# Layer-norm tokens of the MLP turned by transposing DMAs, and VectorE's score row chosen by ScalarE's passes

## The chip, the cores and the metric

The kernel runs on one core of a Trainium2 chip. The metric is the device time of one launch in microseconds (us). The names used are PE for the matmul engine (TensorE), with PEld for its weight loads, DVE for VectorE, ACT for ScalarE, POOL for GpSimd and SP for the engine that issues the DMAs.

## The reference, cut to what matters

One transformer block with adaptive layer norm: 2048 tokens of width 512, 32 heads of width 16, an MLP of width 1376, all in bf16.

```python
mod = (silu(c) @ w_mod).reshape(1, 6, 1, 512)      # sa, ca, ga, sb, cb, gb
h = layernorm(x) * (1 + ca) + sa
q, k, v = split_heads(h @ A_wqkv)
p = softmax(q @ k.T * 16 ** -0.5)
x = x + ga * (merge_heads(p @ v) @ A_wo)
h = layernorm(x) * (1 + cb) + sb                   # the layer norm that the change touches
x = x + gb * (gelu(h @ B_w1 + B_b1) @ B_w2 + B_b2)
```

Attention has 32 x 2048 x 2048 = 134 million exponentials, and that is most of the work.

## The kernel before, in words

**Tiles.** The tokens form four blocks of 512. A run is four heads of one query block: its scores, transposed (128 keys by 512 queries per head), come from matmuls that use 32 rows of the PE array each, so four "rows" 0 to 3 (one per head) can run beside each other. There are 32 runs; each goes over 16 key tiles. The last query block is split in two halves of 256 queries.

**Two makers of exponentials.** ACT takes most scores: `qk_a` fills three PSUM banks, then two, then three (`st`), and one ACT instruction at L852 turns them into bf16 `pt`. These are 626 passes. DVE takes up to four key tiles of a run: `qk_d` lets PE write one head's row (128x512) into one of the two PSUM banks `ax`, and DVE at L900 adds a constant and writes it as int16 `ph`, which read as bf16 is roughly an exponential. Three shifted copies of that (`ph`, `sh`, at L953) and a last one (`sl`, at L932 on DVE and at L938 on POOL) are added up by PE, so that the error averages out. PE multiplies all of these with V (L994, accumulator `od`).

**After a run** `normalise` copies `od` to `OD`, sends the row sums through DRAM with SP's DMAs (`dn`, `dc`, `rn`, `RB`, at L1025 to L1040), and POOL multiplies (`OT`, `OS`, at L1046). When the eight runs of a query block are done, `block_tail` makes the rest of that block: `Wo` (L1155), the residual on DVE (`xb`, L1204), `layer_norm`, `W1` (L1217) with its eviction into `g` or `gp` on DVE (L1221), Gelu on ACT (L1232, L1226), `W2` (L1161), the output sum on DVE (L1244) and SP's store. There are four such tails: three of four token tiles, and one of two tiles, for the first half of the last block. The last two token tiles are made by `last_half`, a chain of its own at the very end.

**The layer norm of a tail** (`layer_norm`, the branch that is not for a tuple of PSUM pools): DVE takes the statistics of each token tile (L599), POOL the reciprocal root, DVE writes the normalised tokens `z` in bf16 (L610, tokens on partitions). PE then turns `z` with an identity matrix: for each of the four 128-wide slices of the width, one transpose per token tile (L672) into an `ax` bank. DVE modulates from PSUM into `h` (tile name `blk`): times 1 + cb, plus sb (L618). `h` is what `W1` reads.

**What sets the order.** The kernel is built by a planner in Python. Each piece of work is an `Op` with an engine, an assumed duration, what it depends on, and a priority. `Plan.step` always commits the operation that can start first on any engine, by assumed times; among those that could start within a small slack of the first, the one with the lowest priority value (`dyn`) goes. So every engine gets a fixed list in the order of the plan, and on the chip each engine runs its list in order, with semaphores. A few rules matter here:
- At most two of `qk_a`'s and two of `qk_d`'s score groups may wait for their maker (`n_a`, `n_d`). `dyn` gives a DVE score 1.0 if none waits and 7.0 if one does; a lower value goes first. An ACT score has 0.0, 2.2 or 6.0.
- Which of a DVE tile's remaining rows is written next is chosen in `Plan.commit` (L190), among `o.rows`.
- Work of the tails on PE gets due times spread over the runs that follow; it goes when nothing pressing is there.
- `SEEDS` (L57) has one number per 12.5 us of planned time. It adds a small pseudo-random term to the priorities, so a different seed gives a different order.
- DVE and POOL operations marked `port=True` are not planned beside each other.
- `heat` adds matmuls on a tile of zeros (L432, L437, L448) where the plan sees PE idle too long.
- DMAs of the planner are all issued by SP, in order.

Of the kernel before, what the change touches and what calls it, by code (L numbers as in the profile page):

```python
# [14 lines left out]
BF16 = mybir.dt.bfloat16  # L15
# [32 lines left out]
PEL = 0.24  # L48
# [5 lines left out]
AL = 0.31  # L54
FILL = 1.6
SPREAD = 0.3
SEEDS = (0, 0, 302, 271, 373, 425, 577, 466, 663, 322, 33, 746, 998, 229, 962, 365, 101, 777, 989, 946, 149, 601, 669, 525, 0, 671, 855, 955, 207, 0, 854, 454, 337, 529, 0, 291, 253, 66, 861, 627, 47, 810, 486, 485, 381, 714, 242, 531, 122, 22, 0, 676, 851, 0, 0, 0, 998, 0, 175, 0, 0, 0, 0, 0, 0, 0)  # L57
HEAT = 1.45


# [39 lines left out]
class Plan:  # L100
# [79 lines left out]
    def commit(self, s, o):  # L180
        self.lists[o.eng].remove(o)
        self.now = s
        if o.acq is not None:
            o.slot = min(range(len(o.acq.free)), key=lambda i: o.acq.free[i])
            o.acq.free[o.slot] = 1e18
            o.tile = o.acq.alloc(o.slot)
        if o.kind == "pv" and s >= self.cool and o.last_left() > 1:
            o.extra, o.us = True, 2 * o.us
        if o.rows is not None:
            o.row = min(o.rows, key=lambda i: self.tiles.get(i, 0.0) if self.mode == "qk" else i)  # L190
            o.mode = ("qk", o.row)
        if o.eng == "PE":
            self.done.append((s, o.act if o.act is not None else (o.us if o.mode[0] != "qk" else o.us * (len(o.mode) - 1) / 4)))
            while self.done[0][0] < s - 30.0:
                self.done.popleft()
            tot = 0.0
            self.fill_at = self.cool = 0.0
            for t, us in reversed(self.done):
                tot += us
                if tot >= HEAT and not self.cool:  # L200
                    self.cool = t + WIN
                if tot >= self.fill:
                    self.fill_at = t + WIN
                    break
            if o.mode[0] != self.mode:
                self.mode, self.tiles = o.mode[0], {}
            for i in o.mode[1:]:
                self.tiles[i] = s + o.us
            self.free["PE"] = s + 0.01
        else:  # L210
            self.free[o.eng] = s + o.us
            if o.port:
                self.port[o.eng] = s + o.us
            if o.eng == "DVE" and o.us > 0:
                self.dve = (s, s + o.us, o.port)
        o.end = s + o.us + o.lat
        if o.kb:
            q = "SP"
            self.bus[q] = max(self.bus[q], s + o.us + 0.9) + o.kb / (300.0 if s < 12.0 else 260.0)
            o.end = self.bus[q] + 0.7  # L220
        if o.fn is not None:
            o.fn(o)
        for owner in o.rel:
            owner.uses -= 1
            owner.last = max(getattr(owner, "last", 0.0), o.end + (DVE_PE if o.eng == "DVE" else 0.0))
            if owner.uses == 0:
                owner.acq.free[owner.slot] = owner.last
        for w in o.waiters:
            w.todo -= 1
            w.ready = max(w.ready, o.end + (DVE_PE if o.eng == "DVE" and w.eng == "PE" else 0.0))  # L230
            if w.todo == 0:
                self.lists[w.eng].append(w)
# [21 lines left out]
def kernel(  # L254
# [94 lines left out]
    def dyn(plan, o):  # L349
        if o.eng == "DVE" and o.run is not None and (  # L350
                o.run < a_run[0] or o.run == a_run[0] and not own[o.run]):
            return 0.05
        if o.eng != "PE":
            return o.prio
        same = (-0.5 if o.mode[0] == plan.mode else 0.0) - 0.2 * o.cont
        if o.kind == "qkA":
            back = n_a[0] - n_a[1]
            return (0.0 if back == 0 else 2.2 if back == 1 else 6.0) + same
        if o.kind == "qkD":
            back = n_d[0] - n_d[1]  # L360
            return (1.0 if back == 0 else 7.0) + same
        if o.kind == "pv":
            if units[0] == NR * NT * 4:
                return 0.0
            few = any(sum(f <= plan.now + 0.3 for f in p.free) <= FEW for p in r_pt)
            return (0.2 if few else 3.0) + same
        if o.kind in urgent:
            return 0.5 + same
        if o.kind == "last":
            return o.prio + 0.1 * same  # L370
        if o.due <= prog():
            return (2.5 if o.due + 16 > prog() else 0.8 if o.due + 48 > prog() else 0.3) + same
        return (4.0 if plan.now >= aux_at[0] else 8.0) + same
# [5 lines left out]
    TAIL, CB = 185, 49  # L379
    TAIL2, TAIL3 = 100, 60  # L380
    plan = Plan(dyn, later)
    plan.need = lambda: plan.free["ACT"] + sum(queued)
    due_now = [1e9, 0.0]

# [242 lines left out]
    def layer_norm(src, deps, mod, mod_dep, hold_z, alloc_h, engines, ps_res, kind, prio,  # L627
                   after=None, nt=TPB):

        ln = op("NIL", None, 0.0, (), lat=0.0, prio=0.0, acq=r_ln)  # L630
        st = [op("DVE", lambda o, t=t: stats(ln, t, src(t)), 0.83, (deps[t], ln, after and after[t]), prio=prio)
              for t in range(nt)]
        rs = [op("POOL", lambda o, i=i: rstd(ln, 2 * i, 2 * i + 2), 1.3,
                 st[2 * i:2 * i + 2] + [o_mh], prio=0.0) for i in range(nt // 2)]
        z = op("NIL", None, 0.0, (rs[0], hold_z), lat=0.0, prio=0.0, acq=r_z)
        za = [op("DVE", lambda o, t=t: apply(ln, z, t, src(t)), 0.33, (z, rs[t // 2]), prio=prio,
                 rel=(ln,), port=True) for t in range(nt)]
        h = op("NIL", None, 0.0, (rs[0],), lat=0.0, prio=0.0, acq=alloc_h)
        done = []
        trs = []  # L640
        if isinstance(ps_res, tuple):
            two = []
            for part in range(2):
                for half in range(2):
                    def tr(o, half=half, part=part):
                        if part:
                            o.tile = two[half].tile
                            two[half].ps = o.tile.bitcast(BF16)
                        ps = o.tile.bitcast(BF16)
                        for j in (2 * half, 2 * half + 1):  # L650
                            for t in (2 * part, 2 * part + 1):
                                nc.tensor.transpose(
                                    out=ps[:, (j % 2) * QB + t * P:(j % 2) * QB + (t + 1) * P],
                                    in_=z.tile[:, t, j * P:(j + 1) * P], identity=ident)
                    one = op("PE", tr, 4 * 0.0705, za[0:2 + 2 * part] + [o_id] + two[half:half + part],
                             lat=PEL, mode=("full", 0), kind=kind,
                             acq=None if part else ps_res[half], rel=(z,))
                    two.append(one)
            trs += two[2:4]
            for half in range(2):  # L660
                one, done_tr = two[half], two[2 + half]
                for j in (2 * half, 2 * half + 1):
                    e = engines[j]
                    done.append(op(e, lambda o, j=j, e=e, one=one: modulate(
                        e, h.tile[:, j, :], one.ps[:, (j % 2) * QB:(j % 2 + 1) * QB], mod, j),
                        0.5 if e == "DVE" else 0.72, (done_tr, mod_dep, h), prio=0.2, rel=(one,)))
        else:
            for j in range(NC):
                def tr(o, j=j):
                    o.ps = o.tile.bitcast(BF16)[:, 0:nt * P]  # L670
                    for t in range(nt):
                        nc.tensor.transpose(out=o.ps[:, t * P:(t + 1) * P],  # L672
                                            in_=z.tile[:, t, j * P:(j + 1) * P], identity=ident)
                one = op("PE", tr, nt * 0.0705, za, lat=PEL, mode=("full", 0), kind=kind,
                         acq=r_ax, rel=(z,))
                trs.append(one)
                e = engines[j]
                done.append(op(e, lambda o, j=j, one=one, e=e: modulate(
                    e, h.tile[:, j, 0:nt * P], one.ps, mod, j), 0.13 + nt * 0.1, (one, mod_dep, h), prio=0.1,
                    rel=(one,)))  # L680
        return h, done, za, trs


# [825 lines left out]
```

## Time and profile before

| | |
|---|---|
| three runs | 776.52, 776.95, 782.23 us (median 776.95) |
| profiled execution, its own time | 780.45 us |
| its span | 778.7 us |
| TensorE clock granted, mean over the span | 0.991 |
| first ACT pass `pt<-st` starts at | 15.1 us |
| PE transposes `ax<-ident,z` at L672 | 56, of 0.219 us each, from 339.3 to 731.9 us |
| DVE modulates of the tails, L618 | 12 of 128x512, 4 of 128x256, all from PSUM |
| Gelu passes over a whole block, L1232 | 3, of 4.9 us, each between two table loads of 1.28 us |
| SP's DMA of a 16x512 row, `qm<-qs` | 0.58 us to issue |

How to read it: a line of a group gives the code line, the engine, the operation, the tile written and the tiles read, the shape, the count, then the busy time, the mean of one instruction in ns, and the idle time of that engine just before these instructions, with what ended it. A line of the view by stretch gives for each engine the busy time and the number of instructions in that stretch, then the granted clock (1.00 is full), the DMA share and GB/s. Instructions on one engine overlap a little, so the step from start to start is shorter than the duration.

### The profile page before, as it was taken

How to read it: one execution, taken by the hardware profiler on the slowest of the kernel's cores; microseconds unless marked ns; L12 is line 12 of the kernel's file. 1: busy time of each engine (PE TensorE's matmuls, PEld its weight loads, DVE VectorE, ACT ScalarE, POOL GpSimd, SP SyncE). 2: the span in 40 equal slices, each digit the busy share in tenths (PEclk: the TensorE clock that was granted, in tenths of full speed). 3: DMA queues.
4: the chain of work that ended last, by engine and by line, in shares of the span. 5: the costliest groups of instructions: out<-in, count | busy, mean ns of one | idle time of the engine just before them, and what ended most of it. 6: DMA issues, size and time to landing. Idle time of an engine off the chain costs nothing.

```text
span 778.7 us, 20637 instructions
## 1 busy us (share of the span) xinstructions
PE 729.6 (94%) x8281; PEld 273.5 (35%) x8281; DVE 715.2 (92%) x1185; ACT 751.0 (96%) x679; POOL 279.4 (36%) x619
## 2 busy tenths in 40 slices
PE   8889989999999899999999999999999899999998
PEld 3433333233243222332322233232334344434454
DVE  6779898999999999999999889979999999998974
ACT  4999999999999999999999999999999999999994
POOL 6222434444433334444444333323234333232320
PEclk9999999999999999999998899999999999999999
DMA  7043001000011101000000100001110000110100
GB/s 216 31 144 85 19 24 44 26 12 16 19 46 51 23 21 50 19 22 28 22 25 17 29 20 23 19 22 31 31 49 24 25 18 18 45 31 11 52 19 28
DMA packets 39074, 28.23 MB, mean 36 GB/s; under 512 B 17957, under 2 KB 34374, under 8 KB 38978
## 3 DMA queue, kind: packets, MB, share of 16 engines
q1 hardware_dynamic: 38970, 26.91, 12.0%
q8 instruction: 65, 1.06, 0.5%
q14 instruction: 31, 0.25, 0.1%
q10 hardware_dynamic: 8, 0.00, 0.0%
HBM read 21.30 MB, written 2.61 MB: 31 GB/s over the span
## 4 chain that ended last, share of the span: by engine, by line
ACT 53%; PE 24%; DVE 12%; issue 9%; DMA 1%; POOL 0%; SPq 0%; DVEq 0%; ACTq 0%
ACT pt L852 52%; PE od L994 8%; PE st L803 7%; DVE ph L900 5%; PE ax L1217 2%; DVE sh L953 2%; PE ax L1161 2%; DVE ph L953 1%; PE t L1161 1%; PE ax L803 1%; PE ax L693 1%; DMA blk<-in_w_mod_dram 1%; DVE xb L1204 1%; PE t L1346 1%; ACT g L1232 1%
## 5 line engine op out<-in xcount | busy, mean ns | idle before, releaser
L852 ACT ACTIVATE pt<-st 128x1536 bf16<-128x1536 f32 x626 | 709.4, 1415 | 6.0 <-PE st L803 4.5
L900 DVE TENSOR_SCALAR ph<-ax 128x512 int16<-128x512 f32 x484 | 318.4, 684 | 23.6 <-PE ax L803 18.8
L938 POOL TENSOR_TENSOR sl<-ph,step 128x128 int32<-128x128 int32 x356 | 163.4, 461 | 335.7 <-DVE sh L953 95.0
L803 PE MATMUL st<-qm,kT 32*128 32x512 bf16 x1564 | 247.7, 385 | 32.7 <-ACT pt L852 26.6
L803 PEld LDWEIGHTS <-kT 32*128 32x128 bf16 x2048 | 86.0, 91 | 247.8 <-issue 237.4
L803 PE MATMUL ax<-qm,kT 32*128 32x512 bf16 x484 | 162.2, 382 | 2.6 <-DVE ph L900 1.7
L994 PEld LDWEIGHTS <-VEB 128*32 128x32 bf16 x4992 | 109.9, 96 | 150.6 <-issue 127.7
L994 PE MATMUL od<-pt,VEB 128*32 128x512 bf16 (+1 forms) x1952 | 149.0, 344 | 0.4 <-DVE OD L1019 0.2
L953 DVE TENSOR_SCALAR sh<-ph 128x4096 int16<-128x4096 int16 x121 | 146.8, 1215 | 1.2 <-PE od L994 0.9
L994 PE MATMUL od<-ph,VEB 128*32 128x512 bf16 (+1 forms) x1216 | 91.6, 341 | 1.3 <-DVE OD L1019 0.5
L994 PE MATMUL od<-sh,VEB 128*32 128x512 bf16 (+1 forms) x1216 | 84.9, 341 | 0.7 <-DVE sh L953 0.6
L953 DVE TENSOR_SCALAR ph<-ph 128x2048 int16<-128x2048 int16 x121 | 83.4, 691 | 0.5
L932 DVE TENSOR_SCALAR sl<-ph 128x1024 int16<-128x1024 int16 (+3 forms) x121 | 58.4, 488 | 0.6
L1046 POOL TENSOR_TENSOR OT<-OD,RB 128x128 bf16<-128x128 f32 x76 | 34.5, 457 | 61.0 <-DVE sh L953 40.7
L994 PE MATMUL od<-sl,VEB 128*32 128x512 bf16 (+1 forms) x608 | 49.1, 342 | 1.9 <-DVE sl L932 1.2
L1217 PE MATMUL ax<-blk,W 128*128 128x512 bf16 (+1 forms) x176 | 43.3, 355 | 0.3 <-DVE ph L900 0.2
L693 PE MATMUL ax<-blk,w 128*128 128x512 bf16 x124 | 36.4, 385 | 2.0 <-DVE blk L618 1.1
L1046 POOL TENSOR_TENSOR OS<-OD,RB 128x128 bf16<-128x128 f32 x48 | 22.8, 478 | 34.3 <-DVE sh L953 11.9
L1221 DVE TENSOR_SCALAR g<-ax,b1c 128x512 bf16<-128x512 f32 x33 | 24.4, 743 | 3.9 <-PE ax L1217 3.8
L1161 PE MATMUL ax<-w,g 128*128 128x512 bf16 x96 | 26.4, 382 | 0.6 <-DVE ph L900 0.5
L599 DVE BATCH_NORM_STATS2 ln_s<-xb 128x6 f32<-128x512 bf16 x32 | 21.7, 677 | 1.3 <-DMA xb<-in_A_x_dram 1.2
L1019 DVE COPY OD<-od 128x512 f32<-128x512 f32 x31 | 21.2, 683 | 0.8 <-PE od L994 0.8
(118 smaller groups left out, 401.1 us busy)
## 6 DMA issues: line engine op xcount, KB each, us to landing
RB<-rn SPq DMA_DIRECT2D x124, 64.0 KB
xb<-in_A_x_dram SPq DMA_DIRECT2D x8, 512.0 KB
out_dram<-o SPq DMA_DIRECT2D x16, 128.0 KB
qm<-qs SPq DMA_DIRECT2D x120, 16.0 KB
W<-in_B_w_dram SPq DMA_DIRECT2D x1, 1376.0 KB
w<-in_A_wqkv_dram SPq DMA_DIRECT2D x3, 384.0 KB
blk<-in_w_mod_dram SPq DMA_DIRECT2D x2, 512.0 KB
xb<-in_w_mod_dram SPq DMA_DIRECT2D x2, 512.0 KB
```

Source lines behind the costliest of these rows:

```text
L693: return chain([(lambda ps, j=j: nc.tensor.matmul(out=ps[:, 0:QB], lhsT=w.tile[:, j, cc * P:(cc + 1) * P], rhs=o_h[b].tile[:, j, :], start ...
L803: nc.tensor.matmul(out=o.tile[:, k * QB:(k + 1) * QB], lhsT=kT[cc][kb][rows, ko * P:(ko + 1) * P], rhs=qm.tile[rows, par, :] if hb is None ...
L852: nc.scalar.activation(out=e.tile[:, 0:len(got) * QB], in_=o.tile[:, 0:len(got) * QB], func=ACT.Exp, scale=ESC)
L900: nc.vector.tensor_scalar(out=ph.tile[:, c0:c0 + QB], in0=o.tile, scalar1=PH_B, scalar2=0.0, op0=ALU.add, op1=ALU.max)
L932: parts = [in_turn(op("DVE", lambda o: nc.vector.tensor_scalar(out=into.tile[:, 0:cols], in0=first.tile[:, 0:cols], scalar1=PH_SH[-1], sca ...
L938: after_dve(nc.gpsimd.tensor_tensor(out=into.tile[:, c].bitcast(I32), in0=first.tile[:, c].bitcast(I32), in1=step, op=ALU.add))
L953: o = op("DVE", lambda o: nc.vector.tensor_scalar(out=dst(o), in0=src(), scalar1=PH_SH[j], scalar2=None, op0=ALU.add), us, deps, lat=DL, p ...
L994: nc.tensor.matmul(out=o_od[r].tile[32 * i:32 * i + 32, n * HB:n * HB + w], lhsT=v_tile(kt)[:, c0:c0 + 32], rhs=got[i][:, at:at + w], star ...
L1046: two = beside(lambda c: nc.gpsimd.tensor_tensor(out=OT.tile[:, c], in0=OD.tile[:, c], in1=o5.tile[:, c], op=ALU.mult), (OT,), (OD, o5))
L1161: nc.tensor.matmul(out=ps, lhsT=g[:, f, col:col + P], rhs=rhs, start=(f == 0), stop=(f == NF - 1))
L1217: mm = chain([(lambda ps, f=f, j=j: nc.tensor.matmul(out=ps[:, 0:N], lhsT=W1[:, j, f * P:(f + 1) * P], rhs=h.tile[:, j, 0:N], start=(j == ...
L1221: ev.append(op("DVE", lambda o, f=f, mm=mm: nc.vector.tensor_scalar(out=g.tile[:, f, 0:N], in0=mm.tile[:, 0:N], scalar1=b1c[:, f:f + 1], s ...
```

## The change

The change has four parts.
- In the tails' layer norm the PE transposes go. For each token tile, one DMA on SP with `transpose=True` reads `z` (128 tokens by 512) and writes the four turned 128x128 pieces into `h`. DVE then modulates `h` in place, in SBUF. That makes 14 transposing DMAs: 4 + 4 + 4 + 2. The `ax` banks are not used for it any more. The planner assumes for the DMAs what it assumes for other DMAs of their size.
- The row of a DVE score is chosen by the time at which the row's part of the PE array is free, and among equals by `rank`: the lowest goes, and that is a row which ACT's next four groups use, the nearest group with the most weight.
- A DVE score that would be the second in waiting gets priority value 4.5, not 7.0.
- The seeds are other numbers.

```diff
-            o.row = min(o.rows, key=lambda i: self.tiles.get(i, 0.0) if self.mode == "qk" else i)
+            o.row = min(o.rows, key=lambda i: (max(s, self.tiles.get(i, 0.0) if self.mode == "qk" else 0.0), self.rank(i)))
...
-            return (1.0 if back == 0 else 7.0) + same
+            return (1.0 if back == 0 else 4.5) + same
...
+    def rank(i):
+        k, n, got = (at["A"][2] + 1) % 4, turn[0], 0.0
+        for w in (1.0, 0.8, 0.6, 0.4):
+            got += w * (i not in [(k + m) % 4 for m in range(SPAN[n])])
+            k, n = (k + SPAN[n]) % 4, (n + 1) % len(SPAN)
+        return got
+    plan.rank = rank
...
+            def turn_(o):
+                for t in range(nt):
+                    nc.sync.dma_start(out=h.tile[:, :, t * P:(t + 1) * P], in_=z.tile[:, t, :], transpose=True)
+            one = dma(turn_, za + [h], kb=nt * P, n=1.4 * nt, prio=0.2, rel=(z,))
             for j in range(NC):
-                def tr(o, j=j):
-                    o.ps = o.tile.bitcast(BF16)[:, 0:nt * P]
-                    for t in range(nt):
-                        nc.tensor.transpose(out=o.ps[:, t * P:(t + 1) * P],
-                                            in_=z.tile[:, t, j * P:(j + 1) * P], identity=ident)
-                one = op("PE", tr, nt * 0.0705, za, lat=PEL, mode=("full", 0), kind=kind,
-                         acq=r_ax, rel=(z,))
-                trs.append(one)
                 e = engines[j]
-                done.append(op(e, lambda o, j=j, one=one, e=e: modulate(
-                    e, h.tile[:, j, 0:nt * P], one.ps, mod, j), 0.13 + nt * 0.1, (one, mod_dep, h), prio=0.1,
-                    rel=(one,)))
+                done.append(op(e, lambda o, j=j, e=e: modulate(
+                    e, h.tile[:, j, 0:nt * P], h.tile[:, j, 0:nt * P], mod, j), 0.07 + nt * 0.066, (one, mod_dep, h),
+                    prio=0.1, port=True))
```

In the `SEEDS` line only the numbers differ.

In the built programs ACT has the same number of instructions, DVE as many evictions and shifts as before, PE the 56 transposes less, 7 more warming matmuls into `ax` and 24 more into `od`. The order of all of them is another one.

More of the change, by code (lines that the diff above doesn't have):

```diff
@@ L56 @@
 SPREAD = 0.3
-SEEDS = (0, 0, 302, 271, 373, 425, 577, 466, 663, 322, 33, 746, 998, 229, 962, 365, 101, 777, 989, 946, 149, 601, 669, 525, 0, 671, 855, 955, 207, 0, 854, 454, 337, 529, 0, 291, 253, 66, 861, 627, 47, 810, 486, 485, 381, 714, 242, 531, 122, 22, 0, 676, 851, 0, 0, 0, 998, 0, 175, 0, 0, 0, 0, 0, 0, 0)
+SEEDS = (0, 62, 0, 205, 94, 455, 281, 215, 174, 199, 958, 663, 0, 0, 59, 926, 0, 38, 893, 459, 43, 311, 545, 477, 23, 854, 395, 682, 778, 249, 233, 206, 159, 855, 709, 762, 0, 909, 558, 0, 43, 798, 487, 758, 482, 947, 255, 935, 722, 822, 354, 19, 0, 0, 0, 450, 439, 0, 735, 603, 0, 0, 0, 0, 0, 0)
 HEAT = 1.45
```

## The prediction

> **What bounds the kernel now.** I read the busy times first, then the groups, then busy time by stretch, then ACT's waits. ACT's passes `pt<-st` (L852) alone are 709.4 us.
>
> ```profile
> PE 729.6 (94%) x8281; PEld 273.5 (35%) x8281; DVE 715.2 (92%) x1185; ACT 751.0 (96%) x679; POOL 279.4 (36%) x619
> PEclk9999999999999999999998899999999999999999
> L852 ACT ACTIVATE pt<-st 128x1536 bf16<-128x1536 f32 x626 | 709.4, 1415 | 6.0 <-PE st L803 4.5
> L900 DVE TENSOR_SCALAR ph<-ax 128x512 int16<-128x512 f32 x484 | 318.4, 684 | 23.6 <-PE ax L803 18.8
> ```
>
> ACT is busy 751.0 of 778.7 us, and before its 626 passes it sat idle 6.0 us in all. By stretch (the columns are PE, PEld, DVE, ACT, POOL, granted clock, DMA share and GB/s):
>
> ```profile
> 0.00:15.00 15.00, 13.15 (x100) 6.33 (x101) 8.26 (x22) 3.80 (x6) 10.49 (x34) 1.00 0.73 213
> 15.00:40.00 25.00, 21.42 (x187) 9.59 (x184) 19.39 (x48) 23.84 (x24) 5.75 (x12) 1.00 0.20 65
> 300.00:400.00 100.00, 95.28 (x956) 30.92 (x953) 98.67 (x161) 100.00 (x90) 43.54 (x95) 1.00 0.08 24
> 400.00:500.00 100.00, 95.90 (x869) 28.70 (x868) 92.74 (x151) 97.00 (x83) 37.86 (x84) 0.93 0.08 22
> 500.00:600.00 100.00, 95.69 (x1066) 33.47 (x1062) 93.68 (x147) 99.94 (x86) 30.56 (x66) 1.00 0.11 31
> 600.00:700.00 100.00, 94.00 (x1440) 42.24 (x1438) 96.09 (x158) 99.48 (x85) 31.98 (x67) 1.00 0.09 26
> 756.00:779.00 23.00, 18.73 (x160) 10.71 (x158) 10.94 (x27) 11.46 (x31) 1.10 (x2) 1.00 0.07 24
> ...
> 415.00:420.00 5.00, 3.68 (x27) 1.13 (x25) 4.96 (x10) 4.97 (x4) 3.16 (x7) 1.00 0.00 0
> 420.00:425.00 5.00, 4.66 (x34) 0.90 (x31) 4.65 (x8) 4.45 (x5) 2.21 (x4) 0.64 0.00 0
> 425.00:430.00 5.00, 5.00 (x33) 0.97 (x32) 2.48 (x7) 3.90 (x4) 0.89 (x2) 0.50 0.01 3
> 430.00:435.00 5.00, 5.00 (x39) 1.42 (x39) 4.20 (x9) 4.04 (x4) 2.26 (x5) 0.50 0.04 10
> 435.00:440.00 5.00, 4.60 (x53) 1.31 (x46) 4.65 (x8) 4.67 (x5) 2.20 (x5) 0.99 0.09 19
> ```
>
> ACT's idle time lies in four places. In the first 15 us it is 11.2 us (loads, layer norm), from 15 to 40 us 1.2 us, after 756 us 11.2 us to the span's end at 778.7 (the closing chain of the last half head). In the 716 us between it is 4.1 us (the same view over all stretches from 40 to 756: 0.00, 0.27, 0.00, 0.00, 3.00, 0.06, 0.52 and 0.28), and 2.9 us of that is one accident: beside the first Gelu pass PE was busy only 3.68 of 5 us, the granted clock then fell to 0.50 for some 14 us, and ACT lost 0.55 + 1.10 + 0.96 + 0.33 us. The profiled execution took 780.45 us, 3.5 above the median of 776.95; without those 2.9 us it would be 777.5, so I read the median as a run without the accident.
>
> So a gain has little room: a run whose ACT never waited between 40 and 756 us would take 780.45 - 4.1 = 776.3. A loss has room: VectorE (DVE) is 93 to 99% busy in these stretches, and PE 93 to 96%, so a wait put on either soon reaches ACT.
>
> **The change part by part.**
>
> Removed: 56 PE transposes `ax<-ident,z` (L672). Sixteen of them took 1.24 us of PE time (that line alone from 338.9 to 344.6 us), so 56 take 4.3 us of 730. PE is ahead of ACT there (two score groups may be in flight), so the saving is not on the path: 0. In the changed order PE gets 7 more warming matmuls into `ax` and 24 more 32-column ones into `od` (104 for 80); these fill pauses: 0. If that cover were gone, PE's net gain would be some 2 us.
>
> Modulates: 16 DVE instructions now read bf16 in SBUF, not PSUM. Two pairs from the timeline (start, duration, then what):
>
> ```profile
> 339.95 0.99 DVE L618 TENSOR_SCALAR blk<-ax,modB 128x512 bf16<-128x512 bf16 x2
> 333.51 0.73 DVE L610 TENSOR_SCALAR z<-xb,mv,rs 128x512 bf16<-128x512 bf16 x2
> ```
>
> The first pair steps by 0.45 us, the second, an SBUF to SBUF pass of the same shape, by 0.33. The price is between 0.33 and 0.45 (no gain); I take 0.33, the same operation and place. Twelve wide and four half-wide ones save 1.5 to 2 us of DVE, off the path: 0.
>
> Added: 14 transposing DMAs on SP, of 128 KB each. Issue: SBUF sources in this trace cost 0.53 (`dn<-OD`) to 0.59 us (`OT<-OS`), so 8 us of an SP that mostly waits. SP runs in order: behind the transposes of the three full tails stand the `dn`, `dc`, `rn` and `RB` of a head's normalisation or a block's output rows. They are not needed before a block's `Wo` product, with OD in two buffers and OT in six, so a few us late cost 0.
>
> The wait added: the first modulate of each tail waits for all its DMAs, and everything behind it on DVE (evictions of score rows, shifts) waits too; PE then finds `ax` full, and ACT finds no scores. Before, the same instruction waited for PE only: 0.4 us once in all. What hides the DMAs is the DVE work between the last `z` and the modulate. In the changed order that is, at this trace's steps from start to start (0.60 us for an eviction or a 128x2048 shift, 1.13 for a 128x4096 one, 0.35 to 0.6 for `sl`):
> - block 0: 2 shifts, 4 evictions, a reciprocal, 2 wide shifts, `qs`: 6.6 us
> - block 1: 3 `sl`, 4 evictions, 3 shifts, an `OD` copy, a wide shift: 7.3 us
> - block 2: 5 evictions, a wide shift, 2 `sl`, an output sum, a shift: 6.4 us
> - last half block: 2 evictions, an output sum, `sl`, a shift, a wide shift: 3.95 us
>
> In the full tails the first two `z` come 9 us or more earlier, so two DMAs are exposed in every tail. With x for one DMA's own time, the path is 2x, plus 1.7 us from an issue to a landing (`dn<-OD` at 358.84, `dc<-dn`, which waits for it, at 360.56). Hidden while x is under 2.3 us in blocks 0 to 2, and under 1.1 us in the last half. No transposing DMA is in the trace. Low end: 128 KB at the 216 GB/s of the first slice, 0.6 us. High end: each of 65,536 elements as a packet; queue q1's 38,970 packets took 12.0% of 16 engines' 778.7 us, 38 ns each, so 65,536 x 38 / 16 = 157 us. Between them: 64-byte pieces, as `dc<-dn` has them, 2,048 x 38 / 16 = 4.9 us. I take 0.6: the source is whole rows of 1 KB, as in `qm<-qs`, the nearest row. Path 2.9 us, hidden everywhere, last half included (1 us spare): 0.
>
> [...]
>
> Row choice, the lower weight of a second waiting DVE score (4.5 for 7.0), new seeds: they reorder PE and DVE everywhere, with the same 626 passes, 484 evictions and 121 shift sets. At best they take ACT's other idle time from 40 to 756 us, 1.2 us; at worst they put a further half-clock stretch in (2.9 us each). I take -0.6, half of the best.
>
> The close: one `gp` eviction (0.4 us step) now stands between the reciprocal and the second transpose of the last head, where before all came ahead; seven more `W1` matmuls (8 took 1.05 us) and eight fewer of PV follow the last score: between -0.3 (the ACT pass set the end anyway) and +0.8; I take +0.5.
>
> Sum: 780.45 - 2.9 (the accident, absent in the median) - 0.6 + 0.5 = **777.5**, that is +0.5 on the median.
>
> **The rivals.**
>
> Slow transposes, on the other side: with x = 4.9 the path is 11.5 us; over the covers 4.9 + 4.2 + 5.1 + 7.6 = 21.8 us. At each place ACT still has up to one two-bank and one three-bank pass (2.2 us by the step of a pair: 709.4 / 313 = 2.27), so 21.8 - 9 = 13: 777.5 + 13 = 790. It decides from x = 2.3 us. For it: nothing in the trace moves columns to partitions by DMA. Against: q1 is 12% busy. [...]
>
> Half-clock stretches: PE has less work of its own around the tails, and Gelu still takes ACT's passes away for 7.5 us three times. Two such stretches, 2.9 us each: 783; three and a short wait behind them: 786. For it: the accident above, and a run of before at 782.23. Against: more warming matmuls, clock 1.00 in all other stretches. [...]
>
> Faster by over 1% needs 769.2 or less: ACT's 751.0, the idle 12.4 of the first 40 us, 11.2 of the close and 1.75 outside the span are 776.35 already. It would take the `W1` work leaving the close altogether and a shorter head: 774 to 775 at best.
>
> **How the numbers follow.** Hidden transposes 0.60 (777.5, own range 774 to 781), slow ones 0.24 (782 to 805), half-clock stretches 0.14 (780 to 787), a real gain 0.02. The range of 773.5 to 790 leaves out the slower half of the slow case and little else. Over 1% is about what a measurement here tells from no change; slower by that (784.7) holds most of the slow case and a third of the clock case: 0.26. Faster 0.02, same 0.72.
>
> **What would show it.** No `ax<-ident,z` in the tails; no wait of DVE `blk<-blk` on a DMA over 1 us; modulates at 0.4, not 0.54 us; ACT's idle before `pt<-st` under 7 us; clock 1.00 beside the Gelu passes. A long DVE idle before `blk<-blk`, with ACT idle behind it at four places, would prove the forecast wrong.

## The result and the profile after

The changed kernel takes 782.65 us (median of 20 runs, 779.67 to 785.51) against 778.0 us before (20 runs, 776.52 to 782.23). The ratio is 1.0053, with a 95% interval of 1.0040 to 1.0067: slower by about 4 us, and by less than one per cent. The forecast was 777.5 us within 773.5 to 790, and "same" at 0.72.

The page of the changed kernel, the lines that answer to those of before:

```profile
PE 728.3 (94%) x8240; PEld 270.5 (35%) x8240; DVE 710.7 (91%) x1185; ACT 751.2 (96%) x679; POOL 279.9 (36%) x626
PEclk9999999999999999999999999999999999999999
L856 ACT ACTIVATE pt<-st 128x1536 bf16<-128x1536 f32 x626 | 709.8, 1379 | 4.5 <-PE st L807 3.3
L904 DVE TENSOR_SCALAR ph<-ax 128x512 int16<-128x512 f32 x484 | 318.6, 686 | 25.0 <-PE ax L807 23.5
```

The 626 passes of ACT and the 484 evictions of DVE are there as before, the clock was 1.00 all through this execution, and ACT waited 4.5 us before its passes instead of 6.0. Yet the span is 778.8 us against 778.7. The profile of before had the half-clock stretch in it, 2.9 us of ACT's time; the changed kernel's has none and needs as long. That is the loss: without its accident the kernel before is some 3 us shorter. The runs say the same. Of the changed kernel's 20 runs four were granted the full clock, and they took 779.67 to 780.71 us, 780.4 in the mean. Beside the first two groups of experiments below the kernel before ran 34 times, 17 of them at a clock of 0.999 or more, and these average 776.9: some 3.4 us less.

By stretch, in the columns of before:

```profile
15.00:40.00 25.00, 20.29 (x190) 9.82 (x187) 19.97 (x49) 22.86 (x23) 5.66 (x12) 1.00 0.20 64
300.00:400.00 100.00, 95.70 (x951) 29.35 (x947) 96.58 (x159) 99.93 (x90) 43.25 (x95) 1.00 0.12 30
400.00:500.00 100.00, 90.99 (x911) 28.03 (x903) 97.54 (x161) 99.70 (x86) 43.69 (x96) 1.00 0.10 24
500.00:600.00 100.00, 96.43 (x1046) 33.57 (x1042) 88.23 (x141) 99.64 (x85) 30.48 (x67) 1.00 0.11 32
600.00:700.00 100.00, 95.36 (x1524) 43.04 (x1522) 97.24 (x157) 99.59 (x86) 33.08 (x72) 1.00 0.13 32
756.00:779.00 23.00, 18.79 (x166) 10.98 (x154) 10.81 (x28) 11.19 (x31) 1.10 (x2) 1.00 0.07 24
```

PE and DVE have more room than before in places (PE is busy 91.0 of 100 us from 400 to 500, DVE 88.2 from 500 to 600). ACT makes nothing of that room. From 300 to 700 us it is busy 99.6 to 99.9 of 100 us, so no large stall has come in, and no gain either.

The transposing DMAs of block 0, first on SP and then the DVE instructions around them (start, duration, what):

```profile
341.31 6.28 SPq L678 DMA_TRANSPOSE blk<-z  x4
347.68 0.53 SPq L1039 DMA_DIRECT2D rn<-dc  x1
```

```profile
342.71 0.73 DVE L618 TENSOR_SCALAR z<-xb,mv,rs 128x512 bf16<-128x512 bf16 x2 [0.59 <-POOL rs L614]
349.92 1.38 DVE L626 TENSOR_SCALAR blk<-blk,modB 128x512 bf16<-128x512 bf16 x4
```

The last `z` is written at 343.44, SP has issued the fourth transposing DMA at 347.59, and DVE modulates at 349.92 without a wait: the line for the modulates carries no idle time. Of the 14 issues the third of this block was the longest, 2.23 us; the median is 1.25. No DVE wait on these DMAs stands anywhere in the changed kernel's trace.

### The profile page after: what moved, and what is told of

Read it like the earlier page. It is cut to its first block, busy times and chain, and to the rows that moved or that the text cites. A ratio compares the mean times of both kernels' runs of the same rounds, so it can differ in the third digit from the quotient of the medians.

```text
span 778.8 us, 20619 instructions
## 1 busy us (share of the span) xinstructions
PE 728.3 (94%) x8240; PEld 270.5 (35%) x8240; DVE 710.7 (91%) x1185; ACT 751.2 (96%) x679; POOL 279.9 (36%) x626
## 4 chain that ended last, share of the span: by engine, by line
ACT 45%; PE 23%; DVE 19%; issue 9%; DMA 2%; POOL 1%; SPq 1%; DVEq 0%; ACTq 0%
ACT pt L856 43%; DVE ph L904 9%; PE od L998 8%; PE st L807 7%; DVE sh L957 3%; DVE ph L957 2%; PE ax L807 2%; PE ax L1221 1%; DVE sl L936 1%; PE t L1165 1%; DMA blk<-in_w_mod_dram 1%; PE ax L697 1%; DVE g L1225 1%; ACT g L1236 1%; PE ax L1165 1%
## 5 line engine op out<-in xcount | busy, mean ns | idle before, releaser
L856 ACT ACTIVATE pt<-st 128x1536 bf16<-128x1536 f32 x626 | 709.8, 1379 | 4.5 <-PE st L807 3.3
L807 PE MATMUL st<-qm,kT 32*128 32x512 bf16 x1564 | 245.6, 382 | 31.5 <-ACT pt L856 24.3
L807 PE MATMUL ax<-qm,kT 32*128 32x512 bf16 x484 | 158.3, 379 | 5.1 <-DVE ph L904 3.2
L998 PE MATMUL od<-pt,VEB 128*32 128x512 bf16 (+1 forms) x1956 | 147.1, 341 | 0.3 <-DVE VEB L633 0.2
L998 PE MATMUL od<-ph,VEB 128*32 128x512 bf16 (+1 forms) x1208 | 90.0, 340 | 2.8 <-DVE OD L1023 2.2
```

Of the source, the lines that this page charges most:

```text
L807: nc.tensor.matmul(out=o.tile[:, k * QB:(k + 1) * QB], lhsT=kT[cc][kb][rows, ko * P:(ko + 1) * P], rhs=qm.tile[rows, par, :] if hb is None ...
L856: nc.scalar.activation(out=e.tile[:, 0:len(got) * QB], in_=o.tile[:, 0:len(got) * QB], func=ACT.Exp, scale=ESC)
L998: nc.tensor.matmul(out=o_od[r].tile[32 * i:32 * i + 32, n * HB:n * HB + w], lhsT=v_tile(kt)[:, c0:c0 + 32], rhs=got[i][:, at:at + w], star ...
```

## The experiments

The question was whether the 4 us come from the transposing DMAs, from the new rule for the row, or from the order of the instructions, which changes everywhere as soon as the planner sees other durations, another rule or other seeds. The third part of the change, the weight, was settled by the built programs alone: with the weight put back to 7.0 the changed kernel's program is the same on every engine, instruction for instruction, and with 4.5 the program of before is the same as before. The weight does nothing.

Four experiments hold the order fixed and change one thing on the chip. In each the lists of PE, DVE, ACT and POOL stay as they were, and SP's too, but for the one that doubles the DMAs. The kernel before, run beside them, took 777.2 us (first group) and 777.5 us (second group).

### The DMAs as plain ones, and issued twice

```diff
 for t in range(nt):
-    nc.sync.dma_start(out=h.tile[:, :, t * P:(t + 1) * P], in_=z.tile[:, t, :], transpose=True)
+    nc.sync.dma_start(out=h.tile[:, :, t * P:(t + 1) * P], in_=z.tile[:, t, :].rearrange("p (j q) -> p j q", j=NC))
```

> The changed kernel in its own order, instruction for instruction, but its 14 transposing DMAs are plain DMAs of the same bytes from z to blk, so h is not turned (this part of the computation is changed). Order theory (the new order of PE and DVE costs the 4 us, the DMAs nothing): the ratio to before stays at 1.004 to 1.007, as the changed kernel's 1.0053. Transpose theory (the DMAs' 1.25 us of issue and their transfers cost the 4 us, through SP or through the memory): a plain DMA issues in about 0.55 us, and the ratio falls to 0.999 to 1.002.

Measured: 782.54 us, ratio 1.0069 (1.0048 to 1.0091), the same as the changed kernel. The DMA lines of the changed kernel and of this one (count, then shortest, median and longest issue in ns):

```profile
L678 SPq DMA_TRANSPOSE blk<-z x14: 1190/1253/2233, 341.3 to 705.2; - x14
```

```profile
L678 SPq DMA_DIRECT2D blk<-z x14: 593/646/719, 340.5 to 705.3; - x14
```

A transposing DMA keeps SP for 1.25 us, a plain one of the same bytes 0.65. The difference, 14 times 0.6 us, is worth nothing in the time. The transposes as such do not cost the 4 us.

```diff
-for t in range(nt):
+for t in [*range(nt), *range(nt)]:
     nc.sync.dma_start(out=h.tile[:, :, t * P:(t + 1) * P], in_=z.tile[:, t, :], transpose=True)
```

> The changed kernel in its own order, but each tail's set of transposing DMAs is issued a second time behind the first (28 DMAs for 14, the same output). Exposed behind the last z are then six DMAs in a full tail, four in the half one: 6 x 1.25 + about 1.7 = 9.2 us against covers of 6.4 to 7.3, and 6.7 against 4. Order theory: DVE waits for DMAs at the four modulates, 2 to 3 us each, and the time grows by 4 to 9 us over the changed kernel (ratio 1.010 to 1.017). Transpose theory: the cost of the DMAs that is there without any wait at the modulates doubles besides, 4 us more (1.015 to 1.022).

Measured: 801.29 us, ratio 1.0307 (1.0271 to 1.0343): more than either theory had. The waits came where they were expected, four of them, of 0.7 to 3.9 us and 10.3 us in all. Block 0 of this kernel, on SP and on DVE, and DVE's waits for these DMAs over the whole run:

```profile
341.06 11.25 SPq L678 DMA_TRANSPOSE blk<-z  x8
352.36 0.57 SPq L1039 DMA_DIRECT2D rn<-dc  x1
```

```profile
349.09 0.68 DVE L904 TENSOR_SCALAR ph<-ax 128x512 int16<-128x512 f32 x1
353.62 1.38 DVE L626 TENSOR_SCALAR blk<-blk,modB 128x512 bf16<-128x512 bf16 x4 [3.85 <-DMA blk<-z]
```

```profile
DVE blk L626 <- DMA blk<-z: 10.3, 4, 3.9
```

SP ends the eighth issue at 352.31, and the modulate starts at 353.62: a transposing DMA has landed, and DVE knows it, 1.3 us after its issue ends (1.3 to 1.4 us at all four waits). So in the changed kernel, by estimate, the last one landed near 347.59 + 1.3 = 348.9, which is 1.0 us before DVE asked for it. That is all the margin there was in block 0. By the same estimate it was 0.8 us in the last half block (issue ended at 706.47, modulate at 708.56) and about 3 us in blocks 1 and 2.

What was wrong in both expectations is the price of such a wait. In block 2 of the same kernel DVE waits from 645.8 to 649.4. The stretches around the end of that wait and behind it (PE, PEld, DVE, ACT, POOL, granted clock; the first one ends where the clock falls):

```profile
648.20:651.60 3.40, 1.32 (x9) 0.37 (x7) 2.22 (x6) 2.77 (x3) 0.62 (x2) 1.00 0.26 67
650.00:655.00 5.00, 2.99 (x29) 0.84 (x32) 5.00 (x10) 1.27 (x3) 1.83 (x4) 0.66 0.03 7
655.00:660.00 5.00, 5.00 (x94) 2.56 (x90) 2.83 (x5) 3.52 (x4) 0.91 (x2) 0.66 0.12 33
```

PE finds `ax` full and stands still from 649.5 to 652.0, until DVE has read a score. In that pause, at 651.6, the granted clock falls to 0.50, and the mean of 0.66 in each of the two slices of 5 us stands for some 3.4 us of half clock in each (after the same wait in block 0 the clock was 0.50 over a whole slice, 355 to 360 us). ACT loses 3.73 + 1.48 = 5.2 us for a DVE wait of 3.6. Over the run, 10.3 us of waits stand against 797.86 - 780.61 = 17.2 us between the two profiled executions and 18.6 us between the medians. SP's later work came late as well (`rn` at 352.36 for 347.68), and its share was not taken apart. PE was busy for 1.32 of the 3.40 us before the clock fell.

### The row rule alone, both ways

The order is planned as it was; only when a DVE score is written is its row chosen by the other rule.

```diff
             o.row = min(o.rows, key=...)          # the plan's own rule, as it was
+            o.er = min(o.emit, key=...)           # the other rule, over the rows not yet written
...
-            qk(o, 0, r, kt, o.row)
+            qk(o, 0, r, kt, o.er)
```

> The changed kernel in its own order on every engine, but which row a DVE score takes is chosen by the old rule when the instruction is written (another row in 226 of 484 scores); the plan goes on as if the new rule held. Row theory (the new rule puts DVE's rows beside the wrong rows of ACT's groups on PE and costs some of the 4 us): the ratio to before falls to 1.001 to 1.003. Order theory (only the new order of instructions costs): it stays at 1.004 to 1.007.

Measured: 784.4 us, ratio 1.0072 (1.0051 to 1.0094). The old rule takes nothing off the loss; whether it adds to it is not shown, since the interval overlaps that of the changed kernel.

> The mirror of it: the kernel before in its own order, with each DVE score's row chosen by the new rule when written (another row in 206 of 484). Row theory: 1.002 to 1.004. Order theory: 0.999 to 1.001.

Measured: 777.52 us, ratio 0.9999 (0.9985 to 1.0012). In the order of before the row that a score takes is worth nothing on the chip, and in the changed order the old row gains nothing. The new rule matters through the order that the planner makes of it.

The second kernel has the order of before, and its profiled execution (span 775.6 us) has only one short half-clock stretch, behind the first Gelu pass, with some 0.6 us of ACT idle time in it, so it is the better one to set beside the changed kernel. ACT's waits from 40 to 750 us, first in the changed kernel, then in this one (total, times, longest):

```profile
ACT pt L856 <- PE st L807: 1.3, 4, 0.4
ACT pt L856 <- PE od L998: 0.4, 1, 0.4
ACT pt L856 <- PE ax L807: 0.3, 1, 0.3
```

```profile
ACT pt L861 <- PE od L1007: 0.6, 2, 0.4
ACT pt L861 <- PE st L812: 0.5, 2, 0.3
ACT pt L861 <- PE ax L812: 0.2, 1, 0.2
```

The span differs by 3.2 us. Where that comes in can be read from the passes, since both kernels have the same 626. From the start of the first to the start of the 276th, first in the changed kernel, then in this one (a view of the tile `pt` alone: PE's matmuls that read it, then ACT's passes):

```profile
15.74:334.25 318.51, 64.97 (x684) 312.41 (x275) 1.00 0.14 41
```

```profile
14.86:331.54 316.68, 65.93 (x684) 311.58 (x275) 1.00 0.15 41
```

The changed kernel takes 1.8 us more here, 0.8 us in passes that last a little longer and 1.0 us in ACT idle time. The kernel with plain DMAs, in the same order, took 318.42 us, and the profile of before 316.67. The first transposing DMA is issued only behind this, at 341.31, so neither the DMAs nor the modulates in SBUF can be the cause, and before that no tail had PE transposes to lose: this part is the order.

From the 276th to the 501st pass the changed kernel takes 270.5 us. The kernel `bend_48` of the next section, which has the order of before up to 608 us and the full clock in this stretch, takes 269.4. These 1.1 us lie where the tails of blocks 0 and 1 are. No wait on a transposing DMA stands there, but the DMAs and the order are not told apart in them. From the 501st pass to the last, with the other two tails and their six DMAs, the changed kernel and `rows_new` differ by 0.1 us, and behind the last pass the close is 0.4 us longer. Together that is 1.8 + 1.1 + 0.1 + 0.4 = 3.4 us, as between the runs at the full clock. The start of the first pass, 15.75 instead of 14.86 us, is left out: the kernel with plain DMAs, in the changed order, starts at 14.99, so this varies from run to run.

### Another order of the same work

```diff
 bend_48:  SEEDS of before, from the 49th number on
-122, 22, 0, 676, 851, 0, 0, 0, 998, 0, 175, 0, ...
+0, 0, 0, 0, 0, ...
 aend_52:  SEEDS of the changed kernel, from the 53rd number on
-0, 0, 0, 450, 439, ...
+0, 0, 0, 0, 0, ...
```

> The kernel before with the seeds from 600 us of planned time on set to 0: the same order up to there, another one behind it, still 626 ACT passes and 121 DVE tiles. Order theory: an order of the same work that was not chosen loses some us in the last fifth: 1.001 to 1.006. Transpose and row theory: nothing of the change is in it, 0.999 to 1.001.

Measured: 780.6 us, ratio 1.0037 (1.0022 to 1.0053). Nothing of the change is in this kernel. The same 626 passes and 121 tiles in another order of the last fifth cost 3 us. Most of it is not in the passes: behind the last one the close takes 25.2 us for 22.8 in `rows_new`, with ACT waiting 5.4 us for PE in the chain of `last_half` instead of 3.1. So an order alone can cost this much, but this one does it in another place than the changed kernel's order.

> The changed kernel with the seeds from 650 us of planned time on set to 0, again 626 passes and 121 DVE tiles; the order differs in the last 90 us. Order theory: 1.003 to 1.011, up or down by a few us against the changed kernel's 1.0053. Transpose and row theory: 1.004 to 1.007, as the changed kernel.

Measured: 784.79 us, ratio 1.0080 (1.0050 to 1.0111). This does not separate the theories; its interval overlaps both forecasts.

### The parts alone, under the planner

With the rest of the change left as it was and the seeds of the one or the other kernel, the planner makes an order that the seeds were not chosen for.

```diff
 no_t:    the changed kernel, with before's PE transposes and modulates from PSUM
 t_only:  the kernel before, with the transposing DMAs and modulates in SBUF
```

> The changed kernel with the PE transposes and the modulates from PSUM put back; row choice, weight and seeds as changed. The planner makes a third order of it. Transpose theory: it comes back to 0.998 to 1.002. Order theory: any order that the seeds were not chosen for loses some us to short waits and half-clock stretches: 1.003 to 1.010.

Measured: 793.75 us, ratio 1.0214 (1.0191 to 1.0236).

> The kernel before with the transposing DMAs alone; row choice, weight and seeds as before. Transpose theory: the whole loss is here, 1.004 to 1.007, with what the new order adds. Order theory: the loss is that of a reordered plan, 1.003 to 1.010, and no DVE wait on a DMA at a modulate; told apart from the first only together with the run with plain DMAs.

Measured: 799.22 us, ratio 1.0294 (1.0271 to 1.0318). Both theories missed both, above all for a reason that the page shows at once. The kernel with the transposes alone:

```profile
L856 ACT ACTIVATE pt<-st 128x1536 bf16<-128x1536 f32 (+1 forms) x631 | 715.3, 1394 | 14.6 <-PE od L998 7.9
L957 DVE TENSOR_SCALAR sh<-ph 128x4096 int16<-128x4096 int16 x118 | 143.9, 1222 | 1.2 <-PE od L998 0.7
```

631 passes of ACT (as in `no_t`), not 626, and 118 shifts `sh`, not 121: DVE had taken three tiles less, and ACT made up for them. With the passes the waits before them grew as well, 14.6 us for 4.5. The split between the two makers is not fixed in the code; DVE starts a tile when the plan finds a buffer free and enough of the run left. A different order shifts it.

The kernel with the transposes alone has a second loss, and the order theory had expected none of its kind: in the last half block DVE waits 1.35 us for the transposing DMAs, PE runs dry behind it, the granted clock is 0.50 from 735 to 740 us, and ACT is idle 3.3 us between 725 and 745. So in an order that gives the DMAs less cover they do cost time.

So the four combinations were built with all seeds 0, where no order is a chosen one.

```diff
-SEEDS = (0, 0, 302, 271, ...)
+SEEDS = (0, 0)
 u000: before; u100: + transposing DMAs; u010: + row rule; u110: both
```

> The kernel before with all seeds 0, so that no order is a chosen one: the built program has 635 ACT passes, not 626 (115 DVE tiles for 121). Order theory, in its sharper form (the order decides how many tiles DVE can take, and a pass costs 709.8 / 626 = 1.13 us): 9 passes are 10 us, with further short waits 1.013 to 1.028.

> The same with the transposing DMAs alone, seeds 0: 632 passes. Order theory: 6 passes, 7 us, 1.009 to 1.024, by the passes 3 to 4 us below the kernel before with seeds 0. Transpose theory (the DMAs cost 4 us of their own): no gain, or above it.

> The same with the new row choice alone, seeds 0: 635 passes, as the kernel before with seeds 0. Order theory: 1.013 to 1.028. Row theory (the rule costs on PE): above the kernel before with seeds 0 by 2 us or more.

> Both, seeds 0 (the weight of the second waiting score changes nothing in the built program): 640 passes. Order theory: 14 passes, 16 us, 1.020 to 1.035, the slowest of the four though each part alone has fewer passes; so the parts have no price of their own. Transpose or row theory: the sum of the two single parts' differences.

| kernel | passes, DVE tiles | median us | ratio to before (95%) |
|---|---|---|---|
| u000 | 635, 115 | 805.26 | 1.0346 (1.0315 to 1.0378) |
| u100 | 632, 117 | 804.19 | 1.0328 (1.0288 to 1.0369) |
| u010 | 635, 115 | 809.24 | 1.0398 (1.0340 to 1.0455) |
| u110 | 640, 112 | 812.22 | 1.0428 (1.0384 to 1.0472) |

All four lie above what the order theory had: a pass costs more than its own 1.13 us. Of the last one, the passes and the shifts:

```profile
L856 ACT ACTIVATE pt<-st 128x1536 bf16<-128x1536 f32 (+1 forms) x640 | 726.6, 1389 | 19.2 <-PE st L807 8.4
L957 DVE TENSOR_SCALAR sh<-ph 128x4096 int16<-128x4096 int16 x112 | 136.0, 1214 | 1.8 <-PE od L998 1.8
```

Its passes are 726.6 - 709.8 = 16.8 us more than the changed kernel's, and the idle time before them 19.2 - 4.5 = 14.7 us more: 31.5 of the 32.4 us between the spans (811.2 and 778.8). Fewer DVE tiles come with more waits, about one microsecond of wait for one of passes. Whether the transposing DMAs gain anything here is not shown: the intervals of u100 and u000 overlap almost wholly. Those of u010 and u000 overlap too, so the row theory's 2 us are neither shown nor excluded by this pair; the two kernels with the row alone have excluded them. That both parts together are slowest agrees with the order theory, but 640 passes for 632 and 635 are a matter of the plan, and the intervals of u010 and u110 overlap too.

## Why the prediction was right, and where its sum was not

The bound was read rightly. ACT's passes set the time, the room for a gain was an ACT idle time of about a microsecond, and no large stall came in. That the median lies in the stated range is in part luck, and the width of that range: 782.65 is outside the 774 to 781 that the favoured case gave itself, and inside the 780 to 787 of the half-clock rival, to which it gave 0.14. From the figures here the sum would be 776.9 (before at the full clock) + 3.0 (order) + 0.4 (close) + 2.3 (half-clock time in the median run) = 782.6.

**The wait added: right in its result, wrong in its size.** The forecast took x = 0.6 us for one DMA's own time and a path of 2.9 us, hidden with 3.7 us to spare in block 0. The cover of 6.6 us was right (343.36 to 349.92 is 6.56). The path was 343.44 to 348.9, 5.5 us, with 1.0 us to spare. A transposing DMA keeps SP for 1.25 us at its issue, the third of this block kept it for 2.23, and SP reached them only at 341.31, behind `dn` and `dc`. A plain DMA of the same bytes took 0.65, so the bandwidth of the first slice was a good figure for the issue of a plain one and half of it for this one. In the last half block the forecast's own limit, x under 1.1 us, was passed; nothing was exposed because the cover there was 4.7 us (703.85 to 708.56) and not 3.95, against a path of 3.9. That the wait was hidden there too is partly luck.

**The price of one DMA.** Four 128x128 blocks in one DMA took 1.25 us to issue and, by estimate, some 2.5 us in all (1.25 and the 1.3 to the landing in the kernel with the doubled DMAs), and several followed each other at 1.25. At the issue that is half as fast as a plain one of the same bytes (0.65), and in the kernel's time no difference shows (ratio 1.0053 with these, 1.0069 with plain ones, the intervals overlapping).

**The PE transposes and modulates: right.** The modulate fell from 536 to 409 ns (2.5 us saved in all, for 1.5 to 2 forecast), PE's and DVE's busy time by 1.3 and 4.5 us, and neither is in the time.

**The order: this step failed.** "Row choice, the lower weight of a second waiting DVE score (4.5 for 7.0), new seeds: ... I take -0.6, half of the best." At the full clock it measured about +3.0 us: 1.8 us before the first transposing DMA, 1.1 us from there to the 501st pass (where a share of the DMAs is not excluded) and 0.1 us behind. The weight and the row itself are worth nothing. The step listed as the worst case only a half-clock stretch. It did not see that an order with the same passes, evictions and shifts can be longer by waits of a few tenths and by slightly longer passes, with the clock at 1.00 throughout.

**The accident: right for before, wrong for the changed kernel.** "I read the median as a run without the accident." The full-clock runs of the changed kernel average 780.4, its median is 782.65: half-clock time costs the median run 2.3 us. The kernel before, in the run of the second group, had 11 of 23 runs at a clock of 0.999 or more (776.9 us in the mean), and its median there is 777.5. The clock was 0.996 or lower in 12 of the changed kernel's 20 runs and in 2 of these 23. So of the 5.1 us between forecast and median, 2.9 us are there at the full clock and 2.3 us are the clock. Where profiles of the two orders show it is the place that the profile of before showed, behind the first Gelu pass: from 420 to 440 us in the order of before (`rows_new`) and in the changed order (`rows_old`),

```profile
420.00:440.00 20.00, 18.56 (x160) 5.56 (x157) 18.59 (x31) 19.45 (x18) 7.98 (x17) 0.91 0.05 12
```

```profile
420.00:440.00 20.00, 18.79 (x188) 5.14 (x188) 18.63 (x33) 18.38 (x17) 7.24 (x16) 0.94 0.07 15
```

with clocks of 0.91 and 0.94 in these two executions. It can happen in both orders; that the changed order makes it more frequent is what the counts above say, and why it does was not taken apart. The forecast also read PE's pause before the fall from the slice of 415 to 420 us, 3.68 of 5 us busy. In the profile of before the clock falls at 421.4, and in the 3.4 us up to there PE was busy 1.91.

**The close: right,** +0.5 forecast, +0.4 measured.

**The rivals.** Slow transposes fell: x is 1.25, not 4.9. Its price was also wrong in kind: it let ACT's queue absorb 2.2 us of each wait, and the doubled DMAs showed a wait of 3.6 us that cost 5.2, with the clock halved behind it. The half-clock rival was half right, as above.

**What stays open:** which of the reordered places make the 1.8 us before the first transposing DMA (they are too small to be told apart one by one), how the 1.1 us behind it divide between the order and the DMAs, why the half-clock stretch is more frequent, and whether seeds chosen further would make the changed kernel faster than before. That was not tried.

## What to carry to other kernels

Where a planner with tuned seeds makes the order, no part of a change can be judged by putting it in or out: hold the order fixed and change only what the instruction does, or compare plans that nobody has chosen. Read first whether the split of work between engines is still the same (here 626 passes and 121 tiles), and only then the waits. Where it is the same, compare the start of each pass in the two traces: a lag that is there before the changed instructions have run at all can't be theirs. Room on two engines that are not the bound was worth nothing here, but a wait put on one of them can cost more than its length: 3.6 us on DVE cost ACT 5.2 in the kernel with the doubled DMAs, where PE ran dry behind the wait and its granted clock fell to 0.50.

## What the runs showed of the hardware that was not expected

- A transposing DMA of 128x512 bf16 from SBUF to SBUF is issued in 1.25 us on SP, a plain one of the same bytes in 0.65, and it has landed 1.3 to 1.4 us after its issue ends (four waits).
- The granted clock fell to 0.50 after stretches in which PE had been busy for part of the time: behind a DVE wait of 3.6 us it had been busy 1.32 of the last 3.40 us, and in the accident of before 1.91 of 3.40. The half clock lasted some 6.8 us in the first case. A run with 10.3 us of such waits was 17 to 19 us longer.
- The DVE copy `modA` (128x8) took 0.17 us in nine profiles and started between 9.36 and 10.02 us in them, and the first ACT pass started between 14.86 (`rows_new`) and 15.78 us (`no_t`). Whether the one comes from the other was not pursued.
